# A table of planned times per task in place of offsets per stage: Fourier filter and gated unit on one core

## The chip, the core and the metric

The kernel runs on one NeuronCore of one Trainium2 chip. Its engines work side by side, each on its own queue in order: TensorE (PE; PEld is its loading of weights), VectorE (DVE), ScalarE (ACT), GpSimd (POOL) and SyncE (SP). POOL and SP only issue DMAs here, but for a few small instructions of POOL. The metric is the device time of one execution in microseconds.

## The reference

```python
X = np.fft.rfft(x, axis=1)                       # x: 8 x 3200 x 256
Y = X * (filt_r + 1j * filt_i)[None, :, :]       # one filter for each channel
x = np.fft.irfft(Y, n=3200, axis=1)
xp = np.concatenate([zeros(8, 4, 256), x], axis=1)
gate = sigmoid(sum(conv_w[k] * xp[:, k:k + 3200] for k in range(5)))
out = (gate * (x @ w_val)) @ w_out               # f32
```

## The kernel before

The transform over 3200 = 100 x 32 points is done as two small transforms, by matmuls with tables that the kernel computes at its start. Each of the 8 batches goes through the same chain of tasks. The code names a task by stage, batch and number: `ib3,0` is the first block of stage `ib` of batch 3.

- `lx` (POOL): loads of x, 8 a batch, f32 to bf16, into 10 buffers. The first batch's loads, the filter's (`f_t`) and the weights' come ahead or in between.
- `s1` (PE, 8 a batch, 2 matmuls): transform over 100. `so` (8): its copy from PSUM to one buffer, by ScalarE or VectorE.
- `t` (VectorE, 4): transpose in blocks of 32, when all `so` are there.
- `s2` (PE, 7; the seventh is half as wide): transform over 32. `xs` (either engine): copy from PSUM. `z` (VectorE): product with the filter. `ia` (PE): inverse over 32. `ue` (either engine): copy from PSUM.
- For batch 0, `k` (4 transposes on VectorE) turns the result. The others go through a scratch buffer in DRAM: `wr` (SP, 7) writes each `ue`, and when all are written `lv` (SP, 8, two DMAs each) loads them back into one buffer `vt`, which the batch before must have left.
- `ib` (PE, 8): inverse over 100. `ye` (ScalarE, 8): copy to `yt`, of which there are two.
- In 7 blocks of 512 points (the last of 128): `cv` (PE): the five-tap filter, 20 matmuls, when all `ye` are there; for batches 6 and 7 a pair of blocks together in 80 small ones. `ga` (ScalarE): sigmoid. `vl` (PE): value product. `gv` (VectorE): gate times value. `op` (PE): output product. `oe` (either engine): copy from PSUM. `st` (SP): store.

PSUM is cut into four slots. A PE task takes one (a pair of `cv` two), and its copy or product frees it.

The order is made on the host, in Python, before the program is built. `Plan.run` plays the kernel through with planned costs (`{"PE": 0.45}` is 0.45 us on PE), landing times of DMAs and counts of buffers. Whenever an engine is free, it gives it the ready task with the smallest key: the task's `rank`, with `stay` added on PE for a task of another shape of array use than the one before, and `lean` added on VectorE for a copy that ScalarE could make too. A copy goes to the engine for which it is picked. The program then issues every engine's instructions in that order, so the order of every queue is fixed, and each instruction waits for its inputs at run time.

`rank` comes from formulas: a stage's offset (`LAG`), one more for batch 0 (`FIRST`), eight for each batch, and `STEP` for each number within the stage. The profile's lines: `so`, `xs`, `ue` and `oe` are L459 on ScalarE and L461 on VectorE; `s1` L468, `t` L487, `s2` L497, `z` L513, `ia` L528, `wr` L551, `lv` L561 and L562, `k` L569, `ib` L579, `ye` L588, `cv` L618 and L632 (pairs), `ga` L642, `vl` L652, `gv` L667, `op` L675, `st` L690.

Of the kernel before, what the change touches and what calls it, by code (L numbers as in the profile page):

```python
# [22 lines left out]

LAG = dict(lx=-461, s1=-523, so=-124, t=307.5, pd=-178, s2=25, xs=106.5, z=302, ia=221,
           ue=176.5, k=-315, ib=312, ye=-498, cv=280, ga=-531.5, vl=-166.5, gv=-478, op=322.5,
           oe=-241.5)
FIRST = dict(lx=-94, s1=139, so=28.5, t=553.5, pd=153, s2=134, xs=-578.5, z=-363, ia=13, ue=-57,
             k=231.5, ib=193.5, ye=245.5, cv=72, ga=-202.5, vl=160, gv=-113, op=346.5, oe=277)
CONV = 1.2
SMALL = (6, 7)  # L30
STEP = dict(lx=0.95, s1=2.5, so=2.05, t=1.9, pd=0.75, s2=1.9, xs=0.25, z=1.15, ia=0.85, ue=2.25,
            k=0.1, ib=0.9, ye=1.65, cv=2.5, ga=2.2, vl=1.2, gv=0.95, op=1.35, oe=0.55)
STAY, LEAN = 32, 139
# [9 lines left out]
class Plan:  # L43
# [5 lines left out]
    def __init__(self, room, slots, stay=1.0, lean=0.0):  # L49
        self.tasks, self.room, self.stay = {}, dict(room), stay  # L50
        self.lean, self.slots = lean, list(range(slots))

    def add(self, name, engines, rank, deps, emit, take=(), give=(), land=0.0, mode=None,
            ps=0, free=()):
        self.tasks[name] = dict(engines=engines, rank=rank, deps=deps, emit=emit, take=take,
                                give=give, land=land, mode=mode, ps=ps, free=free, slots=[],
                                at=len(self.tasks))
# [83 lines left out]
def kernel(  # L141
# [553 lines left out]
    plan = Plan(dict(xt=NXT, so=1, t=1, xs=3, z=3, u=1, e=2, v=1, y=2, g=NGB, gv=NGB, o=NOB), 4,  # L695
# [6 lines left out]
    def dma(name, us, rank, dep, give=(), land=2.3, mode=0):  # L702
        add(name, {"DQ": us}, rank, dep, None, land=land, mode=mode)
        add(name + "+", {"none": 0.0}, rank, [name], None, give=give)

    for b in range(B):
        turned = b in TURN
        t0 = NCH * b

        def at(stage, n=0, b=b, t0=t0):  # L710
            return t0 + LAG[stage] + (FIRST.get(stage, 0) if b == 0 else 0) + STEP.get(stage, 1) * n

        for j in range(NCH):
            if b:
                add(f"lx{b},{j}", {"POOL": 0.6}, at("lx", j), ["hold"],
                    lambda e, b=b, j=j: load_x(b, j), take=("xt",), land=1.5)
                add(f"dx{b},{j}", {"DQ": 1.22}, at("lx", j), [f"lx{b},{j}"], None, land=2.0, mode=1)
            dep = [f"dx{b},{j}"] if b else [f"x0{j}", "cfa"]
            dep = dep + ([f"s1{b},{j - 1}"] if j else [])
            add(f"s1{b},{j}", {"PE": 0.45}, at("s1", j), dep, lambda e, b=b, j=j: s1(b, j),  # L720
                ps=1, take=("so",) if j == 0 else (), give=("xt",), mode=0)
            add(f"so{b},{j}", two(0.93, 1.14), at("so", j), [f"s1{b},{j}"],
                lambda e, b=b, j=j: so(b, j, e), free=[(f"s1{b},{j}", 0)])
        for q in range(4):
            add(f"t{b},{q}", {"DVE": 1.17}, at("t"), [f"so{b},{j}" for j in range(NCH)]
                + ([f"t{b},{q - 1}"] if q else []),
                lambda e, b=b, q=q: turn(b, q), take=("t",) if q == 0 else (),
                give=("so",) if q == 3 else ())
        add(f"pd{b}", {"POOL": 1.2} if turned else {"none": 0.0}, at("pd"),
            ["pool"] + ([f"pd{b - 1}"] if b else []),  # L730
            lambda e, b=b: pad(b), take=("u",) if turned else ("u", "e"))
        for u, (m0, nm) in enumerate(UCH):
            half = 0 if m0 + nm <= FCUT[0][1] else 1
            add(f"s2{b},{u}", {"PE": 0.11 * nm}, at("s2", u), ["wa"]
                + [f"t{b},{q}" for q in range(4)] + ([f"s2{b},{u - 1}"] if u else []),
                lambda e, b=b, u=u: s2(b, u), ps=1, take=("xs", "z"),
                give=("t",) if u == len(UCH) - 1 else (), mode=1)
            add(f"xs{b},{u}", two(0.13 + 0.4 * nm, 0.04 + 0.55 * nm), at("xs", u),
                [f"s2{b},{u}"], lambda e, b=b, u=u: xs(b, u, e), free=[(f"s2{b},{u}", 0)])
            add(f"z{b},{u}", {"DVE": 0.06 + 0.55 * nm}, at("z", u), [f"xs{b},{u}", f"fl{half}"],  # L740
                lambda e, b=b, u=u: zed(b, u), give=("xs",))
            add(f"ia{b},{u}", {"PE": 0.22 * nm}, at("ia", u),
                [f"z{b},{u}", f"te{u // 2},1", f"pd{b}"],
                lambda e, b=b, u=u: inva(b, u), ps=1, give=("z",), mode=1)
            add(f"ue{b},{u}", two(0.13 + 0.4 * nm, 0.04 + 0.55 * nm), at("ue", u),
                [f"ia{b},{u}"], lambda e, b=b, u=u: ue(b, u, e), free=[(f"ia{b},{u}", 0)])
            if not turned:
                add(f"wr{b},{u}", {"SP": 0.45}, at("ue", u), [f"ue{b},{u}"],
                    lambda e, b=b, u=u: wr(b, u), land=1.0)
                dma(f"wq{b},{u}", 0.44 * nm, at("ue", u), [f"wr{b},{u}"])  # L750
        if turned:
            for q in range(4):
                add(f"k{b},{q}", {"DVE": 1.87}, at("k"), [f"ue{b},{u}" for u in range(len(UCH))]
                    + ([f"k{b},{q - 1}"] if q else []),
                    lambda e, b=b, q=q: back(b, q), take=("v",) if q == 0 else (),
                    give=("u",) if q == 3 else ())
        else:
            add(f"wd{b}", {"none": 0.0}, at("ue"), [f"wq{b},{u}+" for u in range(len(UCH))],
                None, take=("v",), give=("u",))
            for j in range(NCH):  # L760
                add(f"lv{b},{j}", {"SP": 0.8}, at("ib", j) - 2, [f"wd{b}"],
                    lambda e, b=b, j=j: lv(b, j), land=1.0)
                dma(f"lq{b},{j}", 0.68, at("ib", j), [f"lv{b},{j}"])
        for j in range(NCH):
            add(f"ib{b},{j}", {"PE": 0.37}, at("ib", j),
# [4 lines left out]
            add(f"ye{b},{j}", {"ACT": 0.79}, at("ye", j), [f"ib{b},{j}"],  # L770
                lambda e, b=b, j=j: ye(b, j), free=[(f"ib{b},{j}", 0)])
        add(f"ha{b}", {"POOL": 0.2}, at("ib"), [f"ye{b},0"], lambda e, b=b: halo(b))
        for c in range(NB):
# [3 lines left out]
            if c == p:  # L777
                add(f"cv{b},{c}", {"PE": CONV if tiny else 1.08 * f}, at("cv", c),
# [4 lines left out]
            add(f"ga{b},{c}", {"ACT": 0.77 * f + 0.16}, at("ga", c), [f"cv{b},{p}"],  # L783
                lambda e, b=b, c=c: gate(b, c), free=[(f"cv{b},{p}", c - p)])
            add(f"vl{b},{c}", {"PE": 0.87 * f}, at("vl", c),
                [f"cv{b},{p}"] + ([f"vl{b},{c - 1}"] if c else []), lambda e, b=b, c=c: val(b, c),
                ps=1, take=("gv",), give=("y",) if c == NB - 1 else (), mode=0)
            add(f"gv{b},{c}", {"DVE": 1.08 * f + 0.06}, at("gv", c),
                [f"vl{b},{c}", f"ga{b},{c}"], lambda e, b=b, c=c: gv(b, c), give=("g",),
                free=[(f"vl{b},{c}", 0)])  # L790
            add(f"op{b},{c}", {"PE": 0.88 * f}, at("op", c), [f"gv{b},{c}"],
                lambda e, b=b, c=c: outp(b, c), ps=1, take=("o",), give=("gv",), mode=0)
            add(f"oe{b},{c}", two(0.77 * f + 0.16, 1.08 * f + 0.06), at("oe", c),
                [f"op{b},{c}"], lambda e, b=b, c=c: oe(b, c, e), free=[(f"op{b},{c}", 0)])
            add(f"st{b},{c}", {"SP": 0.5}, at("oe", c), [f"oe{b},{c}"],
                lambda e, b=b, c=c: store(b, c), land=1.0)
            dma(f"sq{b},{c}", 1.35 * f, at("oe", c), [f"st{b},{c}"], give=("o",))
    add("pool", {"none": 0.0}, -100, [], None, land=20.0)
    add("wts", {"POOL": 5.0}, 8.5, ["hold"], lambda e: load_w())
    for j in range(NCH):  # L800
        add(f"x0{j}", {"none": 0.0}, -100, [], None, land=4.5 + 1.3 * j)
    add("dq", {"DQ": 30.0}, -100, [], None, mode=0)
    for n, when in (("fl0", 27.0), ("fl1", 31.0)):
        add(n, {"none": 0.0}, -100, [], None, land=when)
    add("pc", {"none": 0.0}, -100, [], None, land=1.5)
    add("cfd", {"DVE": 2.0}, -50, ["pc"], lambda e: cf_dve())
    add("cfa", {"ACT": 0.35}, -50, ["cfd"], lambda e: cf_act())
    add("wd", {"DVE": 7.5}, -49, ["cfd"], lambda e: w_dve())
    add("wa", {"ACT": 1.65}, -49, ["wd"], lambda e: w_act())
    add("ey", {"DVE": 0.9}, -48, ["wd"], lambda e: eye())  # L810
    for i in range(len(TCH)):
        add(f"tp{i}", {"PE": 1.2}, 0.5 + 4 * i, ["wa", "ey"], lambda e, i=i: tab_pe(i),
            ps=1, mode=1)
        for w in range(2):
            add(f"te{i},{w}", two(0.65, 0.65), 0.5 + 4 * i, [f"tp{i}"] + (
                [f"te{i},0"] if w else []), lambda e, i=i, w=w: tab_ev(i, w, e),
                free=[(f"tp{i}", 0)] if w else ())
    add("cid", {"DVE": 4.5}, 13, ["t0,3"], lambda e: ci_dve())
    add("cia", {"ACT": 0.35}, 13, ["cid"], lambda e: ci_act())
    add("cim", {"DVE": 0.3}, 13, ["cia"], lambda e: ci_mul())  # L820
    for h in range(2):
        add(f"dg{h}", {"ACT": 1.1}, 10, ["ey"], lambda e, h=h: diag(h))
    add("hold", {"POOL": 0.2}, 0, ["fl1", "pd0"], lambda e: gate_loads())
# [42 lines left out]
```

## Time and profile before

| | us |
|---|---|
| median of three runs | 302.48 (302.35 to 304.95) |
| the profiled execution | 303.88 |
| its span, first to last instruction | 302.1 |
| PE, DVE, ACT busy in it | 261.7, 255.6, 252.6 |
| granted TensorE clock, mean | 0.969 |

The page gives busy times, then the span in 40 slices with each engine's busy share in tenths, then the chain of work that ended last, and groups of instructions by line. A row of a timeline has the start in us, the time it took, engine, line, operation, and in brackets how long the engine had been idle and what ended that. PE's busy time is modelled from pipelined matmuls, so short waits between blocks hide in it. A busy VectorE or ScalarE record begins while the one before it is ending; the distance from start to start is then the price of one more operation.

### The profile page before, as it was taken

Reading aid. Unit: us, or ns where it says so; the run is one execution under the profiler, and the core shown is the slowest. Engines: PE = TensorE matmul, PEld = TensorE weight load, DVE = VectorE, ACT = ScalarE, POOL = GpSimd, SP = SyncE. Lnnn points to the kernel's source line nnn. Section 1 sums busy time; section 2 is a strip of 40 time slices with the busy share of each in tenths; the row PEclk is TensorE's granted clock in tenths of the full one; section 3 lists DMA queues with packets and bytes.
Section 4 is the critical chain, followed back from the end, with each engine's and each line's share of the span. In section 5 each row is a group of like instructions: output and inputs, shape, how many; then the busy total and the mean of one; then the engine's idle time right before and its main releaser. Section 6 shows DMA issues by size and latency. Waiting matters only on the chain.

```text
span 302.1 us, 9397 instructions
## 1 busy us (share of the span) xinstructions
PE 261.7 (87%) x3924; PEld 158.1 (52%) x3924; DVE 255.6 (85%) x284; ACT 252.6 (84%) x301; POOL 59.4 (20%) x123
## 2 busy tenths in 40 slices
PE   2831679889998799999989999999999999999992
PEld 0121426345556435673567456745667667767661
DVE  7788788989999879999999999999998975466471
ACT  3964779999899788998899989999998978877863
POOL 8665457630140041004100400000000000000000
PEclk9999956999999799999999999999999999999998
DMA  6999499999799979799998998748644994885656
GB/s 91 189 163 166 89 175 134 151 189 237 197 252 261 369 187 225 216 330 294 236 278 283 241 249 248 248 177 257 215 160 183 315 326 156 297 289 203 242 203 239
DMA packets 53514, 67.70 MB, mean 224 GB/s; under 512 B 7840, under 2 KB 34336, under 8 KB 53472
## 3 DMA queue, kind: packets, MB, share of 16 engines
q1 hardware_dynamic: 41264, 51.79, 51.5%
q0 software_dynamic: 12208, 15.31, 31.8%
q8 instruction: 31, 0.51, 0.7%
q14 instruction: 11, 0.09, 0.1%
HBM read 42.54 MB, written 38.14 MB: 267 GB/s over the span
## 4 chain that ended last, share of the span: by engine, by line
PE 46%; ACT 18%; DVE 13%; DMA 12%; issue 5%; POOL 4%; ACTq 0%; DVEq 0%; POOLq 0%; SPq 0%
PE ps L675 12%; PE ps L652 10%; PE ps L618 10%; DMA xt<-in_x_dram 5%; ACT yt L588 5%; PE ps L579 4%; DVE gv L667 4%; DVE xs L461 4%; PE ps L528 3%; ACT gt L642 3%; DVE z L513 3%; ACT u L459 3%; PE ps L632 3%; POOL xt L201 2%; DMA f_t<-in_filt_r_dram 2%
## 5 line engine op out<-in xcount | busy, mean ns | idle before, releaser
L667 DVE TENSOR_TENSOR gv<-ps,gt 128x1024 bf16<-128x1024 f32 (+1 forms) x56 | 61.4, 1103 | 19.3 <-PE ps L652 14.7
L513 DVE TENSOR_TENSOR z<-xs,f_t 128x2048 bf16<-128x2048 bf16 (+1 forms) x56 | 62.3, 1140 | 1.9 <-DMA f_t<-f_t 1.4
L642 ACT ACTIVATE gt<-ps 128x1024 bf16<-128x1024 f32 (+1 forms) x56 | 50.9, 939 | 9.2 <-PE ps L618 5.5
L459 ACT ACTIVATE so<-ps 128x1024 bf16<-128x1024 f32 x51 | 49.7, 1031 | 8.2 <-PE ps L468 7.1
L588 ACT ACTIVATE yt<-ps 128x800 bf16<-128x800 f32 x64 | 51.2, 854 | 4.8 <-PE ps L579 4.7
L201 POOL DMA_DIRECT2D xt<-in_x_dram x64 | 35.4, 557 | 96.7 <-PE ps L468 66.2
L468 PE MATMUL ps<-xt,cf_t 100*128 100x512 bf16 x128 | 45.2, 443 | 9.8 <-DMA xt<-in_x_dram 6.7
L652 PE MATMUL ps<-yt,wv_t 128*128 128x512 bf16 (+1 forms) x224 | 52.5, 356 | 0.6 <-ACT xs L459 0.3
L675 PE MATMUL ps<-wo_t,gv 128*128 128x256 bf16 x400 | 51.2, 273 | 1.3 <-ACT yt L588 0.5
L618 PE MATMUL ps<-yt,dg_t 64*64 64x512 bf16 (+1 forms) x880 | 49.3, 357 | 1.3 <-ACT yt L588 1.1
L459 ACT ACTIVATE u<-ps 128x1024 bf16<-128x1024 f32 (+1 forms) x42 | 40.9, 989 | 9.7 <-PE ps L528 9.5
L459 ACT ACTIVATE o<-ps 128x1024 f32<-128x1024 f32 (+1 forms) x41 | 38.0, 938 | 7.1 <-PE ps L675 5.7
L675 PEld LDWEIGHTS <-gv 128*128 128x128 bf16 x400 | 37.2, 98 | 10.6 <-issue 2.9
L487 DVE STREAM_TRANSPOSE tt<-so 128x1024 f32<-128x1024 f32 x32 | 38.3, 1223 | 2.1 <-ACT so L459 2.1
L528 PE MATMUL ps<-z,a_t 64*64 64x256 bf16 x416 | 28.0, 288 | 11.5 <-DVE z L513 8.8
L579 PE MATMUL ps<-ci_t,vt 104*128 104x100 f16 (+1 forms) x512 | 33.5, 212 | 1.7 <-ACT u L459 0.6
L618 PEld LDWEIGHTS <-dg_t 64*64 64x64 bf16 x880 | 24.5, 108 | 18.0 <-issue 5.1
L579 PEld LDWEIGHTS <-vt 104*128 104x128 bf16 (+1 forms) x512 | 28.7, 100 | 10.0 <-issue 5.1
L461 DVE CAST xs<-ps 128x1024 bf16<-128x1024 f32 (+1 forms) x30 | 33.2, 1127 | 0.0
L497 PE MATMUL ps<-tt,w_t 64*64 64x256 bf16 x416 | 23.0, 292 | 8.2 <-DVE tt L487 5.6
L652 PEld LDWEIGHTS <-wv_t 128*128 128x128 bf16 x224 | 19.3, 97 | 17.7 <-issue 3.4
L459 ACT ACTIVATE xs<-ps 128x1024 bf16<-128x1024 f32 (+1 forms) x26 | 24.8, 994 | 3.5 <-PE ps L497 3.3
(98 smaller groups left out, 202.2 us busy)
## 6 DMA issues: line engine op xcount, KB each, us to landing
out_dram<-o SPq DMA_DIRECT2D x48, 512.0 KB
xt<-in_x_dram POOLq DMA_DIRECT2D x64, 200.0 KB, 8.5
escr<-u SPq DMA_DIRECT2D x42, 256.0 KB
vt<-escr SPq DMA_DIRECT2D x56, 192.0 KB
out_dram<-o SPq DMA_DIRECT2D x8, 128.0 KB
f_t<-f_t SPq DMA_DIRECT2D x4, 224.0 KB
escr<-u SPq DMA_DIRECT2D x7, 128.0 KB
vt<-escr SPq DMA_DIRECT2D x56, 16.0 KB
```

What stands on the lines that cost most here:

```text
L201: nc.gpsimd.dma_start(out=xt[0:L], in_=src)
L459: nc.scalar.activation(dst, src, AF.Copy, **kw)
L461: nc.vector.tensor_copy(dst, src)
L468: nc.tensor.matmul(ps[:, 512 * h:512 * h + 512], lhsT=cf_t[0:L].rearrange("p h c i -> p (h c i)"), rhs=xv[:, DQ // 2 * h:DQ // 2 * h + DQ ...
L513: nc.vector.tensor_tensor(z[:, :, :, 0:nm * D], st.pop(("XS", b, u))[:, :, 0:nm * D].unsqueeze(1) .to_broadcast((128, 2, 2, nm * D)), f_t[ ...
L579: nc.tensor.matmul(ps[:, o:o + L], lhsT=v[rows, RC * j + a, 128 * dh:128 * dh + 128], rhs=ci_t[rows, way, :], start=True, stop=True)
L588: nc.scalar.activation(y[:, :, H:H + N].rearrange("p h (a r) -> p h a r", r=R)[:, :, :, RC * j:RC * j + RC], ps[:, :].rearrange("p (h n) - ...
L618: nc.tensor.matmul(ps[o:o + 64, 512 * dh:512 * dh + w], lhsT=dg_t[rows, dh, k, :], rhs=y[rows, dh, BLK * c + k:BLK * c + k + w], start=(k ...
L642: nc.scalar.activation(g[:, :, 0:w], two_banks(ps, w), AF.Sigmoid)
L652: nc.tensor.matmul(ps[:, 512 * eh:512 * eh + w], lhsT=wv_t[:, dh, eh, o:o + 128], rhs=y[:, dh, H + BLK * c:H + BLK * c + w], start=(dh == ...
L667: nc.vector.tensor_tensor(o, i0, i1, op=ALU.mult)
L675: nc.tensor.matmul(ps[:, D * a:D * a + D], lhsT=gv_[:, eh, 128 * a:128 * a + 128], rhs=wo_t[:, c % 2 * pair(b, c), eh, :], start=(eh == 0) ...
```

## The change

The three dictionaries go, and with them the formulas: `rank` is the next entry of a table of numbers, `TIMES`, divided by ten. Each task that stands in an engine's queue has an entry, in the order in which the tasks are added. Tasks without a queue (landings, transfers) have rank 0. `STAY` goes from 32 to 0.4 and `LEAN` from 139 to 1.8. The planned landing times of the filter's two halves go from 27.0 and 31.0 to 27.8 and 32.2. Planned costs, buffers, dependencies and all instructions stay.

```diff
-LAG = dict(lx=-461, s1=-523, so=-124, t=307.5, pd=-178, s2=25, xs=106.5, z=302, ia=221,
...
-FIRST = dict(lx=-94, s1=139, so=28.5, t=553.5, pd=153, s2=134, xs=-578.5, z=-363, ia=13, ue=-57,
...
-STEP = dict(lx=0.95, s1=2.5, so=2.05, t=1.9, pd=0.75, s2=1.9, xs=0.25, z=1.15, ia=0.85, ue=2.25,
...
-STAY, LEAN = 32, 139
+STAY, LEAN = 0.4, 1.8
+
+TIMES = [239, -274, 72, 77, 519, -216, 113, -123, -155, -112, 178, 70, 255, 101, 40, -210, 33,
...
-    def __init__(self, room, slots, stay=1.0, lean=0.0):
+    def __init__(self, room, slots, times, stay=1.0, lean=0.0):
...
-    def add(self, name, engines, rank, deps, emit, take=(), give=(), land=0.0, mode=None,
+        self.lean, self.slots, self.times = lean, list(range(slots)), iter(times)
+
+    def add(self, name, engines, deps, emit, take=(), give=(), land=0.0, mode=None,
             ps=0, free=()):
+        queue = engines.keys() - {"none", "DQ"}
+        rank = next(self.times) / 10 if queue else 0.0
...
-        def at(stage, n=0, b=b, t0=t0):
-            return t0 + LAG[stage] + (FIRST.get(stage, 0) if b == 0 else 0) + STEP.get(stage, 1) * n
...
-    for n, when in (("fl0", 27.0), ("fl1", 31.0)):
+    for n, when in (("fl0", 27.8), ("fl1", 32.2)):
```

In every `add` of a task the argument with the rank goes, and nothing else changes there. What comes out is another order in the queues of PE, VectorE, ScalarE, SP and, in one place, POOL, and another share of the copies between VectorE and ScalarE.

## The prediction

> **What bounds the kernel now.** I read, in this order, the page's busy shares and slices, the stretches of the span with each engine's busy time, VectorE's timeline with its waits, and the orders of both programs, engine by engine. Tasks are named as in the code: `t1,0` is the first transpose of batch 1.
>
> The page, shares and slices (7.55 us each):
>
> ```profile
> PE 261.7 (87%) x3924; PEld 158.1 (52%) x3924; DVE 255.6 (85%) x284; ACT 252.6 (84%) x301; POOL 59.4 (20%) x123
> ...
> PE   2831679889998799999989999999999999999992
> PEld 0121426345556435673567456745667667767661
> DVE  7788788989999879999999999999998975466471
> ACT  3964779999899788998899989999998978877863
> ...
> PEclk9999956999999799999999999999999999999998
> ```
>
> Three engines are within 3% of each other, and no share names the bound. The slices do: PE starts late, VectorE is full until slice 32 and then falls to 4 to 7 tenths while PE stays at 9. The stretches, cut at these turns:
>
> ```profile
> 50.00:110.00 60.00, 53.73 (x740) 30.40 (x741) 54.52 (x51) 54.80 (x65) 16.45 (x32) 0.96 0.95 228
> 110.00:242.00 132.00, 127.04 (x1966) 78.75 (x1966) 128.87 (x121) 122.02 (x142) 11.61 (x25) 1.00 0.82 241
> 242.00:302.10 60.10, 53.60 (x969) 37.18 (x966) 32.27 (x30) 42.69 (x52) 0.10 (x1) 0.99 0.67 245
> ```
>
> (PE, PEld, VectorE, ScalarE, POOL busy; clock; DMA share; GB/s.) From 110 to 242 us VectorE idles 3.1 us of 132. The last spectrum product, `z7,6`, starts on it at 241.9; then PE works off what is left of gate, value and output products to 296.4, with VectorE half idle. So the time is **VectorE's work up to `z7,6`, plus its idle time, plus the PE work that is still queued behind it.** PE is no second bound before that: its queue ahead of `ia7,6` sums to 172 us at the best spacings of the trace, in 243.7.
>
> VectorE's idle time before 242 sits in few places; from the chain of waits, and the timelines of VectorE and PE:
>
> ```profile
> 169.87 3.39 DVE xs L461 x3
> ```
> ```profile
> 49.72 2.37 DVE L487 STREAM_TRANSPOSE tt<-so 128x1024 f32<-128x1024 f32 x2 [1.21 <-ACT so L459]
> ...
> 107.38 2.54 DVE L667 TENSOR_TENSOR gv<-ps,gt 128x1024 bf16<-128x1024 f32 x2 [2.84 <-ACT gt L642]
> ```
> ```profile
> 100.80 0.38 PE L675 MATMUL ps<-wo_t,gv 128*128 128x256 bf16 x2 [0.22 <-ACT yt L588]
> 102.26 4.04 PE L618 MATMUL ps<-yt,dg_t 64*64 64x512 bf16 x40 [1.08 <-ACT yt L588]
> ```
>
> The first row gives the price of a full VectorE operation standing behind another: 3.39/3 = 1.13 us. The longest hole is 2.84 us before `gv1,0`: PE has 0.22 us of work between the last `ib1,7` and `cv1,0`, waits for the eight `ye1`, and then does 40 conv matmuls in 4.04 us, where 20 take 1.08 elsewhere.
>
> **The change part by part.** No instruction is added or removed in kind; VectorE has 229 planned tasks for 227, ScalarE 289 for 291. All that changes is order and which of the two makes a PSUM copy. Before `z7,6` VectorE's copies go from 29 `xs`, 11 `so`, 12 `ue`, 7 `oe` to 15, 20, 17, 4.
>
> 1. *The head, to `t1,0`.* VectorE drops a half copy (`xs0,6`) and swaps the half `ue0,6` for the full `ue0,5`, which is ready sooner; the four `k0` (7.42 us in the timeline) can start at about 40.3 instead of 41.1. Two `so1` copies go between and behind them, 2.27 us into time that ended in the 1.21 us hole above. `t1,0` then starts at 40.3 + 7.3 + 2.3 = 49.9, against 49.7. The load of batch 1's x, which ends this stretch on PE (47.6), is not touched: up to that point POOL's queue is the same. Cost +0.2, and two copies are out of the way.
>
> 2. *From `t1,0` to `gv1,0`.* Work in VectorE's queue: 31 full operations, 12 transposes at 1.16, 4 halves at 0.59 and a quarter at 0.31, 51.7 us, become 32, 12, 3, 1, 52.3 us; measured, 57.7 us with 6.0 idle. In the new order `ue2,5`, `xs2,6`, `ue2,4` and `ia2,5`, `ia2,4`, `z2,4`, `z2,6` stand around the wait for `ye1`, so the 2.84 us hole has other work in it. Whether `gv1,0` itself is earlier depends on batch 1's way through DRAM. Before: last `ue1` ends at 74.9, its write has landed at 79.1, and the loads go out from here to here (SyncE's timeline):
>
> ```profile
> 79.86 0.34 SPq L561 DMA_DIRECT2D vt<-escr  x1
> ...
> 92.05 0.27 SPq L562 DMA_DIRECT2D vt<-escr  x1
> ```
>
> They land from 84.2 to 99.4 (semaphore events), 2.17 us apart; `ib1,7` reads the last one 0.7 us later. In the new order `ue1,6` stands behind 24.6 us of VectorE work from `t1,0` instead of 22.3, so it ends near 77.4. SyncE sends three stores ahead of the loads, and `lv1,2` ahead of `lv1,0`: +2.5 to +4. Against that, three x loads instead of eight compete while the loads run, since five of the `s1` that free x buffers stand behind `ib1,4`. I get the last load at 98.5 to 103 and `gv1,0` at 104.5 (VectorE's work alone) to 110.5. I take 107.4, where it is now, near the middle: the loads may be later, and from `ib1,7` on the new chain needs 6.4 us at full clock where the old one took 7.3. By then 94.9 us of VectorE work is done instead of 92.1.
>
> 3. *From `gv1,0` to `z7,6`.* 93 full, 16 transposes, 8 halves, 5 quarters, 130.3 us, become 91, 16, 7, 6, 127.8 us. Measured: 134.5, so 4.2 idle, which I keep: behind `t_b,3` of batches 4 to 7 stand one to five other operations before the first `xs` or `z` of the batch (two to four now), enough for the 0.5 us that PE needs for the first `s2`. **-2.5 us.** ScalarE takes over the copies: from `ye1,0` to `ye6,0` 135.6 us at back-to-back spacings instead of 133.9, in 156 us; it hides that.
>
> 4. *The tail, from `ia7,6` on PE.* Before: 19 output blocks at 0.87, 17 value blocks at 0.86, 8 conv blocks of 1.08 or 1.28, 16 `ib` at 0.35 and the short ones, 49.2 us, measured 52.7 (3.5 of waits). After: one value block, one `ib` and one conv block less, two `ia` blocks at 0.43 more, 47.8. The waits I keep. **-1.4 us.** The end is the same four output blocks, copies and stores.
>
> 5. *Loads that come closer to their use.* From the last `ue` to `ib`: batch 3 has 22.3 us now and some 13 after (11.8 us of ScalarE's queue), batch 7 has 6.6 us of PE work between `ib6,7`, which frees the load's buffer, and `ib7,0`, and 5.2 after; batch 1's chain needed 9.3 us from `ue` to the first landing. `lv3,1` is now fifth and `lv4,0` last of its batch; batch 4 has 15 us to spare, batch 3 has 0 to 2. Nothing gained at best; at worst 2 us each for batches 3 and 7. PE's waits for these loads now add up to 0.2 us, and I take two such, +0.4.
>
> Sum: -2.5 - 1.4 + 0.4 = -3.5, the 0.2 of the head being inside what fixes `gv1,0`. The profiled execution took 303.88 (span 302.1, 1.8 around it) and would take 300.4; it lies 1.4 above the median of 302.48, so the **forecast is 299.0**.
>
> **The clock.** At 102 to 105.6 the granted clock is 0.50, which is why the 40 conv matmuls took 4.04 instead of 2.16 us. The Trainium skill ("TensorE: Matmul & The Clock Gate", Part 1: The HAM clock gate) says that PE drops to half clock after an idle window of about 3.4 us and gets the full one back after as long a busy one. The length of the dip here agrees with it; the idle time before it does not, PE being busy 1.8 of the 3 us before.
>
> **The rivals.**
> - *The clock stays up and `gv1,0` comes earlier.* With `ia2,5` and `ia2,4` around the wait, PE's gap shrinks; the dip's 1.9 us (4.04 less 2.16) go, `gv1,0` moves to 105.5: **297.1**. Against it: the cover is 0.43 us against a wait of 1.08. Chance 0.20.
> - *The order is too fine for the chip.* Neighbours now rest on planned times of single tasks; planned times miss the 1.28 us table load before the first gate. If VectorE from 110 to 242 idled half-way towards ScalarE's 10.0 us instead of its own 3.1, +3.4 takes the gain back: **302.4**. Chance 0.23.
> - *Slower: the loads are late in batches 1, 3 and 7.* If they land 2.2 us apart behind three stores, `gv1,0` goes to 110.5 (+3.1), and `ib3` and `ib7` wait some 2 us each: -3.5 + 7.1 - 0.4 = +3.2, **305.7**. It decides once `lv1,7` lands after 101, or a load of batch 3 or 7 takes over 8 us. For it: DMA share 0.95 from 50 to 110, and a spare of 0.7 us at `ib1,7`. Against: VectorE has work queued while PE waits. Chance 0.12.
>
> **How the numbers follow.** The forecast has 0.45; from 297.5 to 300.4 is its own spread, some seven tenths of it below 299.5. A measurement of this kernel tells about 1% (3 us) from no change. Faster by over 1%: 0.32 + 0.20 = 0.52. Within: 0.13 + 0.23 = 0.36. Slower: 0.12. The range goes from the clock case with 2.3 of the tail's 3.5 us of waits gone as well, 294.8, to 304.2, which leaves out most of the slow case.
>
> **What would show it.** Right: `z7,6` at about 239.4 on VectorE, no hole over 1.5 us between 62 and 239, `t1,0` at 49.9, PE from `ia7,6` to its end in 51 us. Wrong: waits of PE on `vt<-escr` of over 2 us; a VectorE idle time of over 8 us between 107 and 239; a second dip of the clock.

## The result, and the profile after

The changed kernel took **305.79 us** in the median of 20 executions (302.62 to 307.84), the kernel before 303.07 (300.77 to 307.67) beside it: a ratio of 1.0068, with a 95% interval of 1.0039 to 1.0096. It is slower by 0.4 to 1.0%: by the prediction's own bound of 1% hardly to be told from no change, but on the other side than the forecast of 299.0, and outside the range that ended at 304.2. Ratios leave out executions more than 1.5% above the fastest of their kernel (4 of these 20, and 9 of the 12 of the repetition below), so where a kernel's times spread widely the ratio is below that of the medians. The profiled execution of the changed kernel (302.62, span 300.7) is the fastest of its 20, so its profile shows less than the whole loss. The first experiment below gives a second one, of 308.84, the second longest of 12: the two stand on either side of the medians.

Shares and slices of the changed kernel (7.52 us each):

```profile
PE 255.6 (85%) x3890; PEld 157.9 (52%) x3924; DVE 259.4 (86%) x286; ACT 251.0 (83%) x299; POOL 59.5 (20%) x123
...
PE   2831658599998799999999997999999999999992
...
DVE  7788999689999989999999999799998986666661
...
PEclk9999958699999999999999999999999999999999
```

PE has a hole in its eighth slice (52.6 to 60.1 us), VectorE too, and the clock is low in the sixth and the eighth. The dip near 105 us, which the kernel before had, is gone. (34 records of value products are missing here, hence x3890.) The three stretches:

```profile
50.00:110.00 60.00, 52.05 (x743) 30.16 (x749) 53.80 (x50) 54.42 (x65) 15.41 (x31) 0.94 0.96 221
110.00:242.00 132.00, 125.66 (x1908) 78.32 (x1924) 127.35 (x119) 123.39 (x144) 12.58 (x27) 1.00 0.85 243
242.00:300.70 58.70, 52.58 (x988) 37.36 (x996) 35.44 (x35) 42.51 (x49) 0.10 (x1) 1.00 0.69 254
```

From 50 to 110 VectorE is busy 0.7 us less than before, where 2.8 us more work was to be done by `gv1,0`; from 110 to 242 it idles 4.65 us instead of 3.13. Its timeline says where, and PE's timeline says on what (start, time, engine, and in brackets the idle time before and what ended it). VectorE:

```profile
50.23 4.62 DVE L556 STREAM_TRANSPOSE tt<-so 128x1024 f32<-128x1024 f32 x4
...
55.67 1.23 DVE L530 CAST xs<-ps 128x1024 bf16<-128x1024 f32 x1 [0.82 <-PE ps L566]
...
58.84 1.23 DVE L530 CAST xs<-ps 128x1024 bf16<-128x1024 f32 x1 [1.95 <-PE ps L566]
...
109.22 1.23 DVE L736 TENSOR_TENSOR gv<-ps,gt 128x1024 bf16<-128x1024 f32 x1 [1.01 <-PE ps L721]
...
190.74 1.23 DVE L736 TENSOR_TENSOR gv<-ps,gt 128x1024 bf16<-128x1024 f32 x1 [1.14 <-PE ps L721]
```

PE (L537 is `s1`, L648 is `ib`):

```profile
57.11 1.04 PE L537 MATMUL ps<-xt,cf_t 100*128 100x512 bf16 x2 [1.57 <-DMA xt<-in_x_dram]
...
98.20 1.06 PE L537 MATMUL ps<-xt,cf_t 100*128 100x512 bf16 x4 [1.18 <-DMA xt<-in_x_dram]
...
188.02 0.51 PE L648 MATMUL ps<-ci_t,vt 104*128 104x100 f16 x8 [1.62 <-DMA vt<-escr]
```

The first row is `s12,0`, and it waits for **a load of x**. In the kernel before it began at 53.4. The chain of work that ended last goes through these loads (start, length, what):

```profile
52.41 4.66 DMA xt<-in_x_dram
57.11 1.04 PE ps L537 x2
...
91.15 7.00 DMA xt<-in_x_dram
98.20 1.06 PE ps L537 x4
```

`lx2,0` is issued at 52.4, lands at 57.1 and is used at once; before, it was issued at 39.2 and landed at 48.6. `lx3,5` lands at 98.2 for `s13,5`, which began at 84.7 before. The x load that goes out at 39.2 now is `lx4,7`, which is used at 119.8.

What stands between the places matters too. Behind the first ten of these x loads GpSimd issues the eleven loads of the weights. These rows of its timeline are the first of them and the x loads behind the last:

```profile
41.75 0.77 POOL L343 DMA_DIRECT2D wv_t<-in_moe_w_val_dram  x1 [1.19 <-DMA xt<-in_x_dram]
...
51.86 4.36 POOL L270 DMA_DIRECT2D xt<-in_x_dram  x8
```

The planner has 5.0 us for them (the task `wts`), and they hold the queue for 10.1. `lx2,0` stood ahead of them and now stands behind them, at the twelfth place. Its own transfer, 4.7 us, is a short one; it is late because it is issued late.

That is in the program, and the prediction had not seen it. The comparison of the queues that it went by names an instruction by line, operation and shape, and all x loads have one line and one shape. The section on the change, too, has GpSimd's queue altered in one place only; of its 56 x loads 49 stand elsewhere. By the names of the tasks, the loads of GpSimd's queue stand so (w: the weights; `1,4` is `lx1,4`), where the kernel before has them in the order of their numbers:

```
1,1 1,4 1,2 1,0 1,3 1,5 1,6 1,7 4,7 2,2 w 3,0 2,0 3,1 4,6 2,3 2,1 2,5 4,0 3,6 2,4 2,6 2,7 3,7 3,2 3,4 5,1 3,3 4,5 3,5 ...
```

PE takes the chunks in the order of their numbers: `s1 b,j` is planned behind `s1 b,j-1`. So a chunk whose load goes out late holds all that follow, whose data may lie there already. The same holds for the scratch loads on SyncE (`lv1,2 1,0 1,1 ...`, `lv3,2 3,0 3,5 3,6 3,1 ...`, `lv4,3 4,2 4,5 4,4 4,1 4,6 4,7 4,0`), where `ib` goes by numbers. Each task having its own entry in the table, nothing keeps loads of one batch in order any more; the formula's `STEP` did.

### The profile page after: what moved, and what is told of

The parts are those of the page before. It is cut to its first block, busy times and chain, and to the rows that moved or that the text cites. A ratio compares the mean times of both kernels' runs of the same rounds, so it can differ in the third digit from the quotient of the medians.

```text
span 300.7 us, 9341 instructions
## 1 busy us (share of the span) xinstructions
PE 255.6 (85%) x3890; PEld 157.9 (52%) x3924; DVE 259.4 (86%) x286; ACT 251.0 (83%) x299; POOL 59.5 (20%) x123
## 4 chain that ended last, share of the span: by engine, by line
PE 54%; DMA 24%; ACT 6%; POOL 5%; issue 4%; DVE 3%; SPq 1%; ACTq 0%; DVEq 0%; POOLq 0%
PE ps L744 13%; PE ps L721 12%; PE ps L687 10%; DMA xt<-in_x_dram 10%; DMA vt<-escr 8%; PE ps L648 5%; PE ps L537 5%; PE ps L597 4%; POOL xt L270 3%; PE ps L701 3%; PE ps L566 2%; DMA f_t<-in_filt_r_dram 2%; DMA f_t<-in_filt_i_dram 2%; ACT yt L657 1%; DMA escr<-u 1%
## 5 line engine op out<-in xcount | busy, mean ns | idle before, releaser
L736 DVE TENSOR_TENSOR gv<-ps,gt 128x1024 bf16<-128x1024 f32 (+1 forms) x56 | 61.2, 1106 | 15.5 <-PE ps L721 12.3
L537 PE MATMUL ps<-xt,cf_t 100*128 100x512 bf16 x128 | 43.7, 440 | 13.1 <-DMA xt<-in_x_dram 12.0
L657 ACT ACTIVATE yt<-ps 128x800 bf16<-128x800 f32 x64 | 51.1, 856 | 4.2 <-PE ps L648 2.2
L744 PE MATMUL ps<-wo_t,gv 128*128 128x256 bf16 x400 | 51.9, 273 | 0.6 <-ACT o L528 0.3
L721 PE MATMUL ps<-yt,wv_t 128*128 128x512 bf16 (+1 forms) x190 | 50.1, 353 | 1.8
L528 ACT ACTIVATE so<-ps 128x1024 bf16<-128x1024 f32 x40 | 40.0, 1029 | 13.1 <-PE ps L537 10.4
L687 PE MATMUL ps<-yt,dg_t 64*64 64x512 bf16 (+1 forms) x880 | 50.2, 354 | 0.8 <-ACT yt L657 0.8
L528 ACT ACTIVATE o<-ps 128x1024 f32<-128x1024 f32 (+1 forms) x42 | 40.7, 988 | 7.0 <-PE ps L744 6.2
L528 ACT ACTIVATE xs<-ps 128x1024 bf16<-128x1024 f32 (+1 forms) x41 | 39.3, 983 | 3.5 <-PE ps L566 3.4
L528 ACT ACTIVATE u<-ps 128x1024 bf16<-128x1024 f32 (+1 forms) x35 | 33.5, 960 | 4.4 <-PE ps L597 4.0
L648 PE MATMUL ps<-ci_t,vt 104*128 104x100 f16 (+1 forms) x512 | 32.7, 207 | 4.4 <-DMA vt<-escr 1.9
L648 PEld LDWEIGHTS <-vt 104*128 104x128 bf16 (+1 forms) x512 | 27.6, 97 | 14.3 <-issue 4.7
L530 DVE CAST so<-ps 128x1024 bf16<-128x1024 f32 x24 | 28.8, 1216 | 2.5 <-PE ps L537 2.5
```

The source lines that it names most:

```text
L528: nc.scalar.activation(dst, src, AF.Copy, **kw)
L537: nc.tensor.matmul(ps[:, 512 * h:512 * h + 512], lhsT=cf_t[0:L].rearrange("p h c i -> p (h c i)"), rhs=xv[:, DQ // 2 * h:DQ // 2 * h + DQ ...
L648: nc.tensor.matmul(ps[:, o:o + L], lhsT=v[rows, RC * j + a, 128 * dh:128 * dh + 128], rhs=ci_t[rows, way, :], start=True, stop=True)
L657: nc.scalar.activation(y[:, :, H:H + N].rearrange("p h (a r) -> p h a r", r=R)[:, :, :, RC * j:RC * j + RC], ps[:, :].rearrange("p (h n) - ...
L687: nc.tensor.matmul(ps[o:o + 64, 512 * dh:512 * dh + w], lhsT=dg_t[rows, dh, k, :], rhs=y[rows, dh, BLK * c + k:BLK * c + k + w], start=(k ...
L721: nc.tensor.matmul(ps[:, 512 * eh:512 * eh + w], lhsT=wv_t[:, dh, eh, o:o + 128], rhs=y[:, dh, H + BLK * c:H + BLK * c + w], start=(dh == ...
```

## The experiments

The theories: the x loads out of order cost the time (in the expectations, A), either because a far chunk such as `lx4,7` takes a place and a buffer early (A1), or because the chunks within a batch come out of order (A2); the scratch loads out of order cost it; or neither, and it is the fine order of all the other tasks, which rests on planned times (the rival "too fine for the chip" of the prediction). All kernels compute everything.

The edit of the first group keeps names in the planner's list and sorts the tasks of one stage among the places which that stage has in the queue, leaving all other tasks where the table puts them:

```diff
-            order.append((t["emit"], e, t["slots"]))
+            order.append((n, t["emit"], e, t["slots"]))
...
     order = plan.run()
+    for stage in ("lx",):            # "lv": ("lv",)   "lxlv": ("lx", "lv")
+        at = [i for i, o in enumerate(order) if o[0][:2] == stage]
+        todo = sorted((order[i] for i in at), key=lambda o: [int(v) for v in o[0][2:].split(",")])
+        for i, o in zip(at, todo):
+            order[i] = o
```

**The changed kernel once more, unedited.**

> The changed kernel once more, on the chip of the runs beside it. All theories: near 305.8 us, 0.9% over the kernel before. PE waits for x (in_x_dram) 10 us or more in all and for vt<-escr 3 to 6 us, as in the first profile; if this profile is of a slower execution than the first (302.6), the waits that have grown are the ones that vary.

**x loads in the order of their numbers.**

> The changed kernel with the x loads in natural order (batch, then number) in the same places of GpSimd's queue; every other queue as changed. Theory A, the loads of x issued out of order hold buffers and come late: s12,0 starts at 53.5 to 54 instead of 57.1, waits for x after 40 us fall under 2 us, and the time falls by 3 to 4 us, to 302. Theory B, the loads from scratch (vt<-escr) come late because they stand close to their use and out of order: within 1 us of the changed kernel. Theory C, the order of PE, VectorE and ScalarE is too tight for the chip's durations: within 1 us of the changed kernel.

**Scratch loads of each batch in the order of their numbers.**

> The changed kernel with the scratch loads lv of each batch in natural order in the same places of SyncE's queue; everything else as changed. Theory B: PE's waits for vt<-escr fall under 1 us, time falls by 1.5 to 3 us. Theories A and C: within 1 us of the changed kernel.

**Both.**

> Both kinds of loads in natural order. Theories A and B together: 299 to 301 us, below the kernel before, near the forecast; A alone: 302; B alone: 303 to 304; C: 305 to 306 as changed.

Measured on one chip, beside the kernel before at 302.73:

| kernel | median, us | all executions | ratio to before |
|---|---|---|---|
| unedited (`again`) | 306.80 | 301.0 to 310.6 | 1.0008 (0.9947 to 1.0069) |
| x loads sorted (`lx`) | 300.19 | 299.0 to 301.7 | 0.9911 (0.9876 to 0.9946) |
| scratch loads sorted (`lv`) | 304.18 | 300.8 to 307.3 | 1.0025 (0.9989 to 1.0061) |
| both (`lxlv`) | 297.53 | 296.9 to 299.0 | 0.9829 (0.9786 to 0.9872) |

By medians the x loads' order costs 6.6 us (306.80 less 300.19), the scratch loads' 2.6 (less 304.18), and both together 9.3. By the ratios, which leave out most of `again`, the sizes are smaller. The x loads' order costs 5.9 us with the scratch loads sorted (1.0025 less 0.9829, of 302.73) and 2.9 without (1.0008 less 0.9911). The scratch loads' order costs 2.5 with x sorted (0.9911 less 0.9829), and nothing that shows without (1.0008 against 1.0025). So both orders are shown to cost time, the sizes are known to some us only, and that they add up holds by the medians alone. What is left of the change, with all its other moves, is a gain of 5.2 us over the kernel before, or 1.7%. So the fine order as such is not the loss. And the spread shrinks from 9.6 us (12 executions) to 2.1 (6).

Not all that was expected came. `lx` and `lxlv` fell further than the 302 and the 299 to 301 of their theories, and `s12,0` came to 55.3 in `lx`, not to 53.5 to 54. In `again` PE's matmuls wait 1.9 us for scratch loads, where 3 to 6 were expected.

The spans split by three marks, from the timelines (in each profiled execution):

| | `t1,0` | `s12,0` | `gv1,0` | `gv1,0` to `z7,6` | `ia7,6` to PE's end |
|---|---|---|---|---|---|
| before | 49.7 | 53.4 | 107.4 | 134.5 | 52.8 |
| after | 50.2 | 57.1 | 109.2 | 134.1 | 50.2 |
| `again` | 51.9 | 59.6 | 112.9 | 135.6 | 50.1 |
| `lx` | 50.3 | 55.3 | 106.2 | 135.5 | 50.1 |
| `lv` | 51.1 | 57.9 | 112.0 | 131.9 | 50.1 |
| `lxlv` | 49.8 | 54.8 | 105.4 | 131.9 | 50.1 |

The two costs lie in two stretches. Sorting x moves `gv1,0` (109 to 113 against 105 to 106); sorting the scratch loads shortens what comes behind it by 2 to 4 us. Waits of PE (line, what it waited for; us, times, longest), after:

```profile
PE ps L537 <- DMA xt<-in_x_dram: 12.0, 5, 5.7
...
PE ps L648 <- DMA vt<-escr: 1.9, 2, 1.6
...
PEld L648 <- DMA vt<-escr: 3.5, 4, 2.1
```

and `lxlv`:

```profile
PE ps L537 <- DMA xt<-in_x_dram: 8.8, 6, 5.5
...
PE ps L648 <- DMA vt<-escr: 0.2, 1, 0.2
...
PEld L648 <- DMA vt<-escr: 0.2, 1, 0.2
```

The longest wait for x is the first load of all, in every kernel. Without it, PE waits 6.3 us for x in the profile of after (12.0 less 5.7) and 3.3 in `lxlv`; in `again` it is 8.9 (14.4 less 5.5). Behind 50 us, where the marks move, PE's timeline has two such waits in after (1.57 and 1.18 us, at `s12,0` and `s13,5`), the same two in `again` (2.65 and 1.38), and none in `lxlv`. The scratch loads' price sits at one place: `ib4,0` waits for `lv4,0`, the last of its batch to go out, and VectorE's next `gv` for it. VectorE in `again`:

```profile
195.94 1.23 DVE L736 TENSOR_TENSOR gv<-ps,gt 128x1024 bf16<-128x1024 f32 x1 [3.06 <-PE ps L721]
```

and in `lx`, where the scratch loads are as the table has them:

```profile
189.16 1.23 DVE L736 TENSOR_TENSOR gv<-ps,gt 128x1024 bf16<-128x1024 f32 x1 [1.51 <-PE ps L721]
```

In `lv` and `lxlv` VectorE has no hole over 0.8 us between `gv1,0` and `z7,6`.

**Which part of the x order?** Two further kernels give the x loads by list: `lxb` sorts the chunks inside each batch and leaves every batch its places in the table (so that a load of batch 4 still goes ninth, then `2,0 3,0 2,1 3,1 4,1 ...`); `far1` has all sorted, and `lx4,7` alone brought to the ninth place, with the scratch loads sorted too. And two put one order of the changed kernel into the kernel before, in its own places: the x loads' (`bx`), the scratch loads' (`bv`).

```diff
     order = plan.run()
+    seq = ('10 11 12 13 14 15 16 17 40 20 30 21 31 41 22 23 24 42 32 ...').split()
+    by = {o[0]: o for o in order if o[0][:2] == "lx"}
+    at = [i for i, o in enumerate(order) if o[0] in by]
+    for i, s in zip(at, seq):
+        order[i] = by["lx" + s[0] + "," + s[1]]
```

> The changed kernel with the x loads of each batch in natural order, while the batches keep the places that the table gives them in GpSimd's queue (a chunk of batch 4 still goes ninth, ahead of batch 2); every other queue as changed. Theory A1, chunks of far batches in front of near ones cost the time (places and buffers): 304 to 306 us, as changed. Theory A2, the order inside a batch costs it, since s1 takes the chunks in their numbers: 300 to 301, as with all x loads in natural order. Both in part: 302 to 303.

> The changed kernel with both kinds of loads in natural order (297.5 us), but for one chunk: lx4,7 stands ninth, so that it holds one of ten x buffers until batch 4 and batch 2's chunks go out one place later each. Theory A1: +1 to +3 us, 298.5 to 300.5. Theory A2: within 0.5 us of 297.5.

> The kernel before with its x loads in the changed kernel's order, in the same places; nothing else is changed. Theory A: the loss comes along, +3 to +5 us, 305.5 to 308, with PE's waits for x up by 4 us or more. If the order of x loads only hurts beside the changed order of the other queues: within 1 us of before.

> The kernel before with the scratch loads lv of each batch in the changed kernel's order, in the same places. Theory B needs little room between load and use as well as the wrong order; the kernel before has 10 us and more to spare in batches 3 to 6: within 1 us of before, waits for vt<-escr under 2 us. If the wrong order costs wherever it stands: +1.5 to +3 us.

Measured, beside the kernel before at 303.32:

| kernel | median, us | ratio to before |
|---|---|---|
| sorted inside the batches (`lxb`) | 299.47 | 0.9855 (0.9824 to 0.9886) |
| one far chunk early (`far1`) | 298.65 | 0.9837 (0.9805 to 0.9870) |
| before, x order of after (`bx`) | 322.08 | 1.0608 (1.0569 to 1.0647) |
| before, scratch order of after (`bv`) | 304.45 | 1.0045 (1.0015 to 1.0075) |

`lxb` is no slower than `lx`, though batches are mixed; that speaks for A2, the order inside a batch. `far1` is within its interval of `lxlv`, 0.2 us above it by the ratios. Its 298.65 us lies in the range expected for A1, but the kernel before was 0.6 us slower here than beside `lxlv`, so a price of about 1 us for the one far chunk is not excluded. Most of the loss is A2. `bx` shows that the x order costs by itself, without the table's other moves, but the size was missed: 3 to 5 us were expected and 18.8 measured. Its waits:

```profile
PE ps L468 <- DMA xt<-in_x_dram: 24.9, 9, 6.0
```

and two of them on PE's timeline:

```profile
61.52 1.03 PE L468 MATMUL ps<-xt,cf_t 100*128 100x512 bf16 x2 [3.78 <-DMA xt<-in_x_dram]
...
94.85 1.41 PE L468 MATMUL ps<-xt,cf_t 100*128 100x512 bf16 x4 [3.99 <-DMA xt<-in_x_dram]
```

Without the first load PE waits 18.9 us for x, where the kernel before waits 1.1 (6.7 less 5.6): the 17.8 between them are nearly the whole loss. `gv1,0` is at 121.5 there, 14.1 us later than before. In the table's own order the `s1` stand where the planner expects the loads, `s13,5` at 98.2 for example; in the kernel before they stand earlier (84.7), so the same order of loads meets them sooner. That reading was not tried further. `bv` costs 0.5 to 2.3 us by its interval: more than nothing, and less than the 2.5 to 2.6 that sorting the scratch loads gives back in the changed kernel. Its 1.1 us by medians lie between the two ranges that were expected.

**The best version, with its yardstick.** `lxblv` sorts the x loads inside the batches and the scratch loads; `lxlv_b` is `lxlv` again.

> The changed kernel with the x loads of each batch and the scratch loads of each batch in natural order, the batches of x in the places of the table. If the order inside a batch is the whole loss: 296.5 to 298, as with all loads in natural order or a little below (x loads sorted inside batches alone gave 299.5, sorted throughout 300.2). If the table's placing of whole batches still costs: 298.5 to 300.

> The same kernel as lxlv, on the chip of the run beside it, as its yardstick: 297 to 298, ratio to the kernel before 0.98 to 0.985.

| kernel (before: 303.19) | median, us | ratio to before |
|---|---|---|
| `lxblv` | 297.57 | 0.9817 (0.9778 to 0.9855) |
| `lxlv_b` | 297.97 | 0.9837 (0.9803 to 0.9872) |

No difference between them, and both beat both kernels. PE's waits for x in `lxblv` are 5.7 us without the first (11.1 less 5.4), nearly those of after, at 8 us less time: a sum of waits is not yet a price. What counts, as far as these traces go, is where they stand: of the 5.7 us all but 1.7 (at `s12,2`) fall before 50 us.

## Why the prediction was wrong, step by step

The profile of `lxlv`, which is the change without the two orders of loads, is the one to hold against the steps; its stretches:

```profile
50.00:110.00 60.00, 55.46 (x783) 33.32 (x782) 57.04 (x53) 57.41 (x68) 16.21 (x32) 0.97 0.98 229
110.00:242.00 132.00, 128.54 (x2005) 80.97 (x2004) 128.05 (x120) 124.77 (x146) 11.61 (x25) 1.00 0.86 253
242.00:295.60 53.60, 47.08 (x886) 32.94 (x883) 30.30 (x29) 37.48 (x43) 0.10 (x1) 0.97 0.66 244
```

and VectorE's two marks:

```profile
105.35 1.22 DVE L736 TENSOR_TENSOR gv<-ps,gt 128x1024 bf16<-128x1024 f32 x1 [0.95 <-PE ps L721]
...
237.25 0.69 DVE L582 TENSOR_TENSOR z<-xs,f_t 128x1024 bf16<-128x1024 bf16 x1
```

- **Step 1, the head.** `t1,0` at 49.9 was right (50.2 in after, 49.8 in `lxlv`). Its sentence on the loads, "up to that point POOL's queue is the same", was wrong, and this is **the step that failed**: the first eight loads are those of batch 1 in both programs, but in another order, and from the ninth on nearly every place holds another chunk. The cost is not in the head but behind it, and no term of the sum, and none of the three rivals, has loads of x in it. Step 2 has them only as competitors of the scratch loads. They were counted as one kind, by line, and not looked at by name. So the price of their order was put at nothing; it is 6.6 us by medians and 3 to 6 by ratios.
- **Step 2, `gv1,0`.** 107.4 was taken, from 104.5 to 110.5. After has 109.2 and `again` 112.9; `lxlv` 105.4. The 2.84 us hole did get other work (1.01 left in after, 0.95 in `lxlv`), and the clock, at 0.50 from 102.35 to 105.76 before, is full there in both. So the rival "the clock stays up", with `gv1,0` at 105.5 and 297.1 us, is what the change would have been without the two orders of loads: 105.4 and 297.5. That the total fits as well is in part luck, since the tail gave more than its sum had (step 4).
- **Step 3, from `gv1,0` to `z7,6`.** 2.5 us less were forecast, so 132.0. `lxlv` has 131.9: right. After has 134.1 and `again` 135.6, for the scratch loads.
- **Step 4, the tail.** 51 was forecast for the 52.7 measured there (52.8 in the table's marks). After has 50.2 and `lxlv` 50.1: the direction held, and 2.7 us were gained instead of 1.4 to 1.7. With 47.8 us of work, as the prediction counted it, 2.3 to 2.4 of the 3.5 us of waits that were kept are left.
- **Step 5, scratch loads.** They were seen as a danger, at the right place ("`lv3,1` is now fifth and `lv4,0` last of its batch"), and then mis-sized: 0.4 us was taken, and about 2.5 is measured with x in order. Batch 3 waits 0.3 at `ib3,1`. Batch 4 was said to have "15 us to spare", and it is `lv4,0` that PE waits for. In after `ib3,7` at 172.25 is the last to read the buffer; SyncE then issues the eight loads from 172.8 to 185.1, 12.3 us for what the planner has as eight tasks of 0.8, and the last one lands at 187.9. Nothing was left of the 15 us, since the load that goes out last is the one that is needed first.
- **The rival "too fine for the chip"** expected VectorE to idle 3.4 us more from 110 to 242. After has 1.5 more. It is 0.8 more in `lxlv`, whose `z7,6` starts at 237.2 already, so that tail work lies in that stretch: the order of single tasks held on the chip, but for loads.
- **The rival "slower", 305.7,** had the measured time and the wrong mechanism: late scratch loads in batches 1, 3 and 7. With x in order and the scratch loads as they are, `lx` is faster than before.
- **The signs of being wrong** that the prediction named would not have found the x loads. In after PE's matmuls wait 1.9 us for scratch loads and VectorE idles 5.7 us from 107 to 239, both within the bounds; only a second dip of the clock came, at 54.5.
- One count of the prediction is misread, and nothing hangs on it: VectorE's copies "before `z7,6`" are those from `t1,0` on. From the start, 30 `xs`, 13 `so`, 14 `ue` and 7 `oe` become 15, 24, 19 and 4.

On the sum: in spans, `lxlv` gains 2.0 to `gv1,0`, 2.6 to `z7,6` and 2.7 in the tail, and gives 0.8 back in between and behind: 6.5 (302.1 to 295.6; by medians the gain is 5.2, since the profiled execution of before lies above its median). The forecast had 3.5 of it. The orders of the loads take 9.3 by medians away again, 5 to 7 by ratios.

Why loads in the table's order are late on the chip is shown in part. It is not that a load takes longer than planned: the planner, run with the table, lands the 56 x loads of batches 1 to 7 in 5.5 to 11.7 us from their issue, with a median of 6.9, and in the profile of after they take 3.6 to 10.4, with a median of 6.8. They go out later than planned: `lx2,0` at 52.4 instead of 44.1, for the most part behind the weights, and `lx3,5` at 91.2 instead of 85.9. The plan leaves 2.35 us and 0.2 us for these two. What makes `lx3,5` go out late was not taken apart. In after `lx1,0`, `lx2,0`, `lx2,1` and `lx3,5` land with 0.2 us to spare or less; so do several chunks of batch 1 in the kernel before, so that this alone is no sign of a loss.

## What to carry to other kernels

When a change rewrites the order of an in-order queue, list the queue by the names of the data, not by line and shape: loads of the same form can be permuted without showing, and a consumer that takes them in order then waits for the last of them (3 to 6.6 us here, 18.8 us in the kernel before). A search on single tasks needs the loads of one tile kept in the order of their use; planned costs as they are measured (the weights took 10.1 us for 5.0) may help too, which was not tried. A few lines that sort the loads turned 0.7% slower into 1.7% faster.

## What the runs showed that was not expected

**In these traces the clock changes on a grid of 3.41 us.** Between the head and the last microseconds, the granted clock is 0.50 from 102.35 to 105.76 us in the kernel before, from 54.46 to 61.29 in after, and from 58.97 to 65.80 and 192.09 to 195.50 in `again`: each time for 3.41 us or twice that, and the 126.29 us between the two dips of `again` are 37 times 3.413. After, cut at these turns (PE, PEld, VectorE, ScalarE, POOL busy; granted clock; DMA share; GB/s):

```profile
51.05:54.46 3.41, 1.88 (x32) 1.40 (x29) 3.41 (x4) 3.41 (x6) 3.41 (x7) 1.00 0.71 79
54.46:57.87 3.41, 1.40 (x10) 0.32 (x10) 1.61 (x2) 1.40 (x2) 1.87 (x5) 0.50 0.97 157
57.87:61.29 3.42, 3.42 (x38) 1.53 (x38) 2.36 (x2) 2.69 (x3) 0.55 (x1) 0.50 1.02 183
```

The clock falls at 54.46, before the wait for `lx2,0` (55.54 to 57.11) begins; PE was busy 1.88 of the 3.41 us ahead, waiting for copies and for `t1`. The wait for x lies in the second stretch, behind which the clock stays low for 3.4 us more: the conv block that starts at 58.51 takes 2.34 us, where 20 matmuls take 1.25 to 1.27 later in the same trace. So that stretch may be the wait's second price; that it would else have been at full clock is not shown. The longest idle time of PE there is 1.57 us. The Trainium skill ("TensorE: Matmul & The Clock Gate", Part 1: The HAM clock gate) has the clock fall after an idle window of about 3.4 us; as near 105 us in the kernel before, PE was not idle for that long in one piece, and the measured falls stand against taking it as one unbroken gap.

**The same wait costs this only sometimes.** At `ib4,0` PE waits 1.62 us in after and 1.99 in `lx`, and the clock stays at 1.00 behind it. In `again` it waits 1.88, and then (PE's timeline):

```profile
191.57 0.52 PE L648 MATMUL ps<-ci_t,vt 104*128 104x100 f16 x8 [1.88 <-DMA vt<-escr]
191.92 1.75 PE L744 MATMUL ps<-wo_t,gv 128*128 128x256 bf16 x8
193.46 0.87 PE L648 MATMUL ps<-ci_t,vt 104*128 104x100 f16 x8
194.13 1.71 PE L721 MATMUL ps<-yt,wv_t 128*128 128x512 bf16 x4
```

with a granted clock of 0.50 from 192.09 to 195.50; in after the last three take 1.04, 0.52 and 1.03. That is 1.7 us more for the same wait, and the 3.06 us hole of VectorE above instead of 1.14. Where the wait falls on the grid differs: in `again` it lies whole in one stretch (188.68 to 192.09, PE busy 1.53 us), in after it is cut in two at 187.58, which is 54.46 plus 39 such stretches (2.18 us busy in the stretch to there). A limit on the busy time does not come out of it: in `lx` PE is busy 1.79 of the 3.41 us to 188.24, and the clock stays. What decides whether it falls was not settled. It may bear on the spread, since the changed kernel goes from 301.0 to 310.6 and the one with sorted loads from 296.9 to 299.0; this is one execution, and no run tests it.
